# One half-load of V on ScalarE's queue, w_h ahead of the first rows of q, X's transposes ahead of a matmul group, and one half addition on GpSimd

## The chip, the cores and the metric

The kernel runs on one core of one Trainium2 chip. The core has five engines that run side by side and are tied together by semaphores: TensorE (PE, matmuls; its weight loads are shown apart as PEld), VectorE (DVE), ScalarE (ACT), GpSimd (POOL) and SyncE (SP), which here only issues transfers. Transfers between the chip's memory (HBM) and the core's own memory (SBUF) run on 16 DMA engines. They are issued from three queues: SP's, ACT's and POOL's. A load that changes the type on its way is issued from POOL.

The metric is device time in microseconds (us), the median of several executions, with the range beside it. One execution is also recorded by a profiler; its trace gives the start and length of every instruction.

## The reference

The reference is a windowed attention followed by a highway layer, in float32:

```python
keep = (pos_k < 4) | ((q_pos - k_pos >= 0) & (q_pos - k_pos < 128))
a = softmax(where(keep, q @ k.T / 8, -1e9))     # batch 4, heads 8, sequence 768, head size 64
x = (a @ v) as [3072, 512]                       # batch and sequence, heads side by side
H = maximum(x @ w_h, 0)
T = 1 / (1 + exp(-(x @ w_t + b_t)))
out = T * H + (1 - T) * x
```

Every query sees at most 128 keys up to itself, and the first four keys (the sinks).

## The kernel before

The 3072 rows are 24 tiles of 128 rows, six for each of four batches; a tile holds all 8 heads. For tile n these stages run:

- **scores** (`masks`, `product`, line 341): PE writes q times k of all heads, for the tile's keys and this and the next tile's queries, into one PSUM tensor `ps_s`, which is used again for every tile.
- **expo** (449): ACT takes the exponential of all of it into `E[n]`.
- **values** (460, 463): PE multiplies `E[n-1]` and `E[n]` with `v_of(n-1)` and `v_of(n)`, V in 16 bit with a column of ones, into `ps_av`.
- **norm** (480, 482): DVE divides by the sums and writes `X[n]`.
- **x_transpose** (498) and **x_copy** (503): PE transposes `X[n]` in four pieces into another part of `ps_av`, ACT copies them to `XT[n]`. For some tiles **sink_scores** (362), the scores of the sinks for several tiles, go into `ps_av` too, between the transposes and the copy.
- **gate** and **tanh** (508, 516): PE multiplies `XT[n]` with w_t into `ps_z`, ACT takes the tanh; **gate_value** (520 or 523) makes the sigmoid of it.
- **hidden** and **diff** (529, 542): PE multiplies `XT[n]` with w_h into `ps_h`, DVE computes max(H, 0) - X into `DD[n]`. There is one `ps_h`, so `hidden` of one tile waits for `diff` of the tile before.
- **gated** (547) multiplies `DD[n]` with the gate on DVE, **added** (553) adds X, on POOL for most tiles and on DVE for the last ones, and **store** (557) sends the tile out.

The stages of several tiles are interleaved by hand in one loop over n: turn n does scores and expo of tile n, values, norm and transposes of tile n-1, and gate and hidden of tile n-2. The order in which the program issues the instructions is the order on each engine (`_keep_traced_order`): an instruction that waits holds up all behind it on its engine, the issues of transfers among them.

Before q and k can be multiplied they are loaded by POOL in 16 bit into `nat` (`load_part`, line 117), in parts of 32 partitions, four parts (g = 0 to 3) to a segment of q or k, and DVE transposes a segment in blocks into `tr` (`transpose_qk`, line 133). The parts of batch 1's first segment are four of q (the first issued ahead of the loop, the others in turn 2) and four of k (turn 2). Their transposes stand in turns 4 (q) and 5 (k), and the scores of tile 6, the first of batch 1, need both.

V is loaded in 32 bit by SP, one transfer of 256 KB to a tile (`load_v`, line 140), into one of eight buffers; in turns up to 5 the transfer waits for the last matmul of the turn's scores (`after`). A cast brings V to 16 bit: on DVE for tiles 0 to 5 (`cast_v`, line 150), later mostly on POOL. V of tile 4 is loaded in turn 3, cast in turn 4 and used by `values(4)` in turn 5.

w_t and w_h are one transfer each on POOL's queue; w_h (line 644) is issued just ahead of the loop, behind the first part of batch 1's q (line 643). Its first user is `hidden(0)`, which turn 4 holds.

In turn 4 the order is: scores, `expo(4)`, `gate_value(0)`, `values(3)`, `norm(3)`, `gate(2)`, `tanh(2)`, `hidden(0)`, `diff(0)`, the transpose of batch 1's q, `cast_v(4)`, `gated(0)`, `added(0)`, more loads, then `x_transpose(3)`, `sink_scores` and `x_copy(3)` (lines 716 to 735). Turn 5 has the scores of tile 5 first, then `hidden(1)`, then `values(4)`.

After the loop the last tiles are finished one after the other. The last tile, 23, is done in two halves of 256 columns (lines 787 to 802): for each half gate, tanh, gate_value, hidden, diff, gated and `finish` (added and store). The left half is stored by SP, the right by ACT. Between the two, tile 22 is summed on PE and copied by ACT (line 798), and SP stores it (line 799).

Of the kernel before, what the change touches and what calls it, by code (L numbers as in the profile page):

```python
# [37 lines left out]
def kernel(  # L38
# [83 lines left out]
    def load_rows(b, i, which, gs=range(G)):  # L122
        for g in gs:
            load_part(b, i, g, which)
# [9 lines left out]

    V32 = [None] * N

    def load_v(n, after=None):
        b, t = divmod(n, NC)
        V32[n] = work.tile([P, H, D], FP32, tag="V32", name="V32", bufs=8)
        ins = sp.dma_start(out=V32[n],  # L140
                           in_=v[b, :, t * P:(t + 1) * P, :].transpose([1, 0, 2]))
        if after is not None:
            tc.add_manual_dep(
                ins.ins, after.ins.name,
                mybir.DependencyInfo(
                    mybir.DependencyClass.Sync, mybir.DependencyReason.DATA),
                reason="behind the loads needed first")

    def cast_v(n, engine):
        engine.tensor_copy(out=v_of(n)[:, :, 0:D], in_=V32[n])  # L150
# [144 lines left out]
    def sink_values(b, heads=slice(0, H)):  # L295
        if heads.start == 0:
            pool.tensor_copy(out=vs32[64:P, b, 0:D], in_=vs32[0:64, b, 0:D])
        shape = [P, heads.stop - heads.start, D + 1]
        pool.tensor_tensor(
            out=vs[b][:, heads], in0=vs32[:, b].unsqueeze(1).to_broadcast(shape),  # L300
            in1=vmask[:, heads].unsqueeze(2).to_broadcast(shape), op=ALU.mult)
# [101 lines left out]
    def opening(n, n1, n0):  # L403
        t = n1 % NC if n1 is not None else -1
        first = 0 if t >= 4 else 2
        todo = []

        def columns(half):
            b, c = divmod(n, NC)
            q1 = 2 * P if c + 1 < NC else P  # L410
            return q1 - K2 if half else min(q1, 2 * P if c == 0 else 3 * K2)

        for g in range(G):
            for half in range(2):
                split = n0 is not None and n is not None and 7 <= n < N - 1
                when = 256 if split and g == first + 1 - half else 0
                for u in range(4) if n is not None else ():
                    todo.append((when, len(todo), product, (n, u, g, half)))
                    when += columns(half)
                if n0 is not None and g == first + half:  # L420
                    if not split:
                        todo.append((when, len(todo), bias, (n0, g, half, 0)))
                    todo.append((when + 10 * P if split else when + 256, len(todo),
                                 bias, (n0, g, half, 1)))
                if t >= 2 and g // 2 == 1 - first // 2:
                    todo.append((when + 1 if split else when + 257, len(todo), sinks, (n1, g % 2, half)))
        ahead_of = []
        if n is not None:
            masks(n)
            for half in range(2) if n0 is not None and 7 <= n < N - 1 else ():  # L430
                ahead_of.append(bias(n0, first + 1 - half, half, 0))
        if ahead_of:
            passed = act.nop()
            behind(passed, ahead_of[-1])
        last = None
        for _, _, function, args in sorted(todo, key=lambda x: x[:2]):
            ins = function(*args)
            last = ins if function is product else last
            if function is bias and ahead_of:
                behind(ins, passed)  # L440
        return last
# [198 lines left out]
    cast_v(0, dve)  # L640
    sink_keys(0, dve)
    sink_values(0)
    load_rows(1, 0, 0, range(1))
    pool.dma_start(out=wh, in_=moe_w_h.rearrange("(kc p) of -> p kc of", p=P))

    idle(18)
    last = N - 1
    for n in range(last):

        nb, n1 = n - 2, n - 1  # L650
        joined = n < 5 or n >= 7
        before = (n1 if 0 <= n1 < N else None, nb if nb >= 0 else None)
        if n < N:
            after = opening(n, *before) if joined else scores(n)
            expo(n)
            if n in (4, 5):
                gate_value(n - 4)
            if n > NC and n % NC == NC - 1:
                gate_value(n - 3)
            for m in v_at.get(n, ()):  # L660
                if m < N:
                    load_v(m, after if n < 6 else None)
            if n % NC == (3 if n < NC else 1) and n // NC + 1 < B:
                load_sinks(n // NC + 1)
        if 5 <= n <= 6:
            hidden(1 if n == 5 else 3)
        if n == 0:
            idle(5)
        if not joined:
            opening(None, *before)  # L670
        if 0 <= n1 < N:
            values(n1)
        for m in cast_by_pool.get(n, ()):
            cast_v(m, pool)
        if n in late:
            finish(late[n])
        if NC <= n < N and n % NC == 0:
            sink_keys(n // NC)
        if n == 2:
            load_rows(1, 0, 0, range(1, G))  # L680
            load_rows(1, 0, 1)
        if n > NC and (n + 2) // NC < B and n % NC >= NC - 2:
            half = n % NC - (NC - 2)
            sink_values((n + 2) // NC, slice(G * half, G * half + G))
        if n != 4:
            load_parts(n)
        if n == NC + 1:
            sink_values(1)

        done = list(completed.get(n, ()))  # L690
        if n == 6:
            store(0)
            complete(done.pop(0))
        turn = list(units.get(n, ()))
        if 5 <= n <= 6:
            diff(1 if n == 5 else 3)
        if n == 7:
            cast_v_alone(7)
        if 0 <= n1 < N:
            norm(n1)  # L700
        if n == 3:
            transpose_qk(0, 2, 1, slice(0, 1))
            transpose_qk(0, 2, 1, slice(1, 2))
        if n == 2:
            transpose_qk(0, 2, 0)
        if n == 1:
            transpose_qk(0, 1, 1)
        if 0 < n < 4:
            cast_v(n, dve)
        for unit in turn if n != 4 else ():  # L710
            transpose_qk(*unit)

        if nb >= 0:
            gate(nb)
            tanh(nb)
        if n == 4:
            hidden(0)
            diff(0)
            transpose_qk(*turn.pop())
            cast_v(n, dve)  # L720
            gated(0)
            added(0)
            load_parts(n)
        if n == 5:
            gate_value(2)
            hidden(2)
        if n == 1:
            idle(3)
        if 6 <= n <= N:
            hidden(nb, range(KC // 2))  # L730
        if 0 <= n1 < N:
            x_transpose(n1)
            if n in sinks_at:
                sink_scores(*sinks_at[n])
            x_copy(n1)
            if n in sinks_at:
                sink_expo(*sinks_at[n])
            if nb >= N - 4:
                gate_value(nb)
        if 6 <= n <= N:  # L740
            hidden(nb, range(KC // 2, KC))
        if n in ahead:
            gate_value(ahead[n], pool)
        if n == last - 1:
            cast_v(last, pool)
        for m in done[:-1]:
            complete(m)
        if n == 5:
            diff(2)
            cast_v(n, dve)  # L750
        if 6 <= n <= N:
            diff(nb)
        for m in done[-1:] if n < last - 1 else ():
            complete(m)
# [32 lines left out]
    for part, cols, h, queue in ((0, left, h_left, sp), (1, right, ps_h[:, right], act)):  # L787
        gate(last, cols, gate_of(last, part))
        tanh(last, cols, gate_of(last, part))
        gate_value(last, cols=cols)  # L790
        hidden(last, cols=cols, into=h)
        if part == 1:

            for i, x in enumerate((flat(X[last - 1], slice(0, DM)), DD[last - 1])):
                pe.matmul(o_sum, lhsT=ident, rhs=x, start=(i == 0), stop=(i == 1),
                          skip_group_check=True)
            O[last - 1] = work.tile([P, DM], FP32, tag="O", name="O")
            act.copy(out=O[last - 1], in_=o_sum)
            sp.dma_start(out=out[(last - 1) * P:last * P, :], in_=O[last - 1])
        diff(last, cols, h)  # L800
        gated(last, cols)
        finish(last, cols, dve, queue)

    _keep_traced_order(tc)
# [33 lines left out]
```

## Time and profile before

| | |
|---|---|
| median of three runs | 106.77 us (106.72 to 108.35) |
| the profiled execution, its own time | 107.31 us |
| its span, first to last instruction | 105.3 us |
| PE busy | 94.1 us, 89% of the span |
| DVE busy | 86.4 us, 82% |
| ACT busy | 80.0 us, 76% |
| POOL busy | 83.5 us, 79% |
| read from HBM, written | 21.05 MB, 6.29 MB |

The rows that the next part quotes are of these kinds. A row of the timeline has the start in us from the span's start, the length in us, the engine and line, the operation with what it writes and reads, how many such instructions follow each other, and in brackets the idle time of the engine just before, with what ended it. Engine names with a q (SPq, ACTq) are issues of transfers. A row of transfers has what is moved, the queue, the count, KB of each and the median time in us from issue to landing. A row of queues has packets, MB and the time that the packets took, as a share of 16 engines' time in that window. A row of groups has the operation, its count, and after the bar the total busy time in us, the mean in ns, and the idle time before. Matmuls are pipelined and their ends modelled: consecutive matmuls overlap in the rows.

### The profile page before, as it was taken

The page shows a single profiled execution, that of the slowest core. Times are in us where ns is not written, and L with a number is a line of the kernel's source. Part 1 is how long each engine was busy: PE and PEld are TensorE (multiplying, and loading weights), DVE is VectorE, ACT ScalarE, POOL GpSimd, SP SyncE. Part 2 cuts the span into 40 slices and gives each one's busy share as a digit, 9 for nine tenths or more (in the row PEclk, how much of TensorE's full clock was granted, in tenths as well). Part 3 has the DMA queues.
Part 4 walks back from the last instruction along what each step waited for, and adds up shares of the span by engine and source line. Part 5 has one row for each costly group of instructions (what it writes and reads, how often), then busy time and mean ns, then how long its engine had stood idle before and what let it go on. Part 6 is the DMA issues. An engine that isn't in the chain of part 4 may idle for free. (4 is left out here: it accounts for less than half of the span.)

```text
span 105.3 us, 4691 instructions
## 1 busy us (share of the span) xinstructions
PE 94.1 (89%) x1960; PEld 52.4 (50%) x1960; DVE 86.4 (82%) x189; ACT 80.0 (76%) x105; POOL 83.5 (79%) x140
## 2 busy tenths in 40 slices
PE   5966786888999999999999999999999999999930
PEld 2323363454555545655565565554665656464610
DVE  6888755564896999899988996899889979999960
ACT  3297588687967499789778996897689978976750
POOL 6899709964998998897999999989978869768000
PEclk9999999999999999999999999999999999999995
DMA  2999999799999999989989999999996966252523
GB/s 54 229 237 238 185 207 224 99 175 197 230 222 253 209 261 202 182 163 207 237 188 219 203 217 230 207 241 283 219 242 157 270 187 218 106 199 103 202 93 107
DMA packets 36388, 20.81 MB, mean 198 GB/s; under 512 B 27020, under 2 KB 32912, under 8 KB 36368
## 3 DMA queue, kind: packets, MB, share of 16 engines
q1 hardware_dynamic: 29216, 13.31, 47.6%
q0 software_dynamic: 6848, 6.82, 42.0%
q10 hardware_dynamic: 304, 0.39, 1.3%
q8 instruction: 15, 0.25, 1.0%
q14 instruction: 5, 0.04, 0.2%
HBM read 21.05 MB, written 6.29 MB: 260 GB/s over the span
## 5 line engine op out<-in xcount | busy, mean ns | idle before, releaser
L449 ACT ACTIVATE E<-ps_s,ebias 128x2048 f16<-128x2048 f32 (+1 forms) x24 | 43.8, 1825 | 12.0 <-PE ps_s L341 12.0
L133 DVE STREAM_TRANSPOSE tr<-nat 128x384 f32<-128x384 f32 (+2 forms) x29 | 26.4, 937 | 1.6 <-DMA nat<-in_q_dram 1.2
L529 PE MATMUL ps_h<-wh,XT 128*128 128x512 f16 (+1 forms) x96 | 27.2, 375 | 0.5 <-DMA wh<-in_moe_w_h_dram 0.5
L553 POOL TENSOR_TENSOR O<-DD,X 128x512 f32<-128x512 f16 x19 | 22.0, 1157 | 5.6 <-DVE DD L547 3.8
L117 POOL DMA_DIRECT2D nat<-in_k_dram x40 | 21.8, 548 | 3.7 <-DMA wt<-in_moe_w_t_dram 2.6
L508 PE MATMUL ps_z<-wt,XT 128*128 128x512 f16 (+1 forms) x96 | 24.2, 374 | 0.1
L117 POOL DMA_DIRECT2D nat<-in_q_dram x32 | 17.8, 560 | 3.2 <-DMA wh<-in_moe_w_h_dram 2.2
L542 DVE SCALAR_TENSOR_TENSOR DD<-ps_h,X 128x512 f16<-128x512 f32 (+1 forms) x24 | 16.2, 674 | 4.8 <-PE ps_h L529 4.3
L341 PE MATMUL ps_s<-tr 32*64 32x192 f16 (+3 forms) x768 | 16.0, 243 | 2.5 <-DVE tr L133 2.3
L482 DVE TENSOR_TENSOR X<-ps_av,rec 128x512 f16<-128x512 f32 x23 | 15.9, 692 | 0.8
L516 ACT ACTIVATE TH<-ps_z 128x512 f16<-128x512 f32 (+1 forms) x24 | 14.0, 581 | 2.4 <-PE ps_z L508 2.4
L503 ACT COPY XT<-ps_av 128x512 f16<-128x512 f16 x23 | 13.5, 586 | 2.7 <-PE ps_av L498 1.1
L463 PE MATMUL ps_av<-v,E 128*128 128x65 f16 x184 | 13.5, 194 | 0.2 <-DVE v L150 0.2
L379 PE MATMUL ps_z<-brow,ones 32*64 32x256 f16 x94 | 12.7, 278 | 0.1
L341 PEld LDWEIGHTS <-tr 32*64 32x64 f16 x768 | 10.8, 104 | 3.7 <-DVE tr L133 2.0
L529 PEld LDWEIGHTS <-XT 128*128 128x128 f16 x100 | 8.7, 98 | 7.0 <-issue 1.0
L460 PE MATMUL ps_av<-v,E 128*128 128x65 f16 x152 | 12.0, 194 | 0.0
L463 PEld LDWEIGHTS <-E 128*128 128x128 f16 x192 | 11.7, 97 | 0.5
L460 PEld LDWEIGHTS <-E 128*128 128x128 f16 x160 | 10.2, 97 | 3.2 <-issue 1.8
L150 POOL CAST v<-V 128x512 f16<-128x512 f32 x17 | 11.3, 665 | 0.0
L508 PEld LDWEIGHTS <-XT 128*128 128x128 f16 x100 | 8.3, 98 | 5.9 <-issue 0.4
L547 DVE TENSOR_TENSOR DD<-DD,TH 128x512 f16<-128x512 f16 (+1 forms) x23 | 9.8, 427 | 0.8
(91 smaller groups left out, 112.4 us busy)
## 6 DMA issues: line engine op xcount, KB each, us to landing
V<-in_v_dram SPq DMA_DIRECT2D x24, 256.0 KB, 6.3
out_dram<-O SPq DMA_DIRECT2D x23, 256.0 KB, 3.1
nat<-in_k_dram POOLq DMA_DIRECT2D x24, 64.0 KB, 5.0
nat<-in_q_dram POOLq DMA_DIRECT2D x16, 96.0 KB, 4.7
nat<-in_k_dram POOLq DMA_DIRECT2D x16, 96.0 KB, 4.4
nat<-in_q_dram POOLq DMA_DIRECT2D x16, 64.0 KB, 5.5
first<-in_q_dram SPq DMA_DIRECT2D x6, 128.0 KB, 4.2
wt<-in_moe_w_t_dram POOLq DMA_DIRECT2D x1, 512.0 KB, 7.8
```

Source lines behind the costliest of these rows:

```text
L117: engine.dma_start(out=into[32 * g:32 * g + 32].rearrange("p hg m d -> p hg (m d)"), in_=(q, k)[which][b, :, t0:t0 + nt, :].rearrange("(hg ...
L133: dve.transpose(out=dst, in_=src)
L341: return pe.matmul(ps_s[ks, g, hg, q0:q1], lhsT=tr[b][rows, 1, hg, k0:k0 + K2, e], rhs=tr[b][rows, 0, hg, c * P + q0:c * P + q1, e], start ...
L449: act.activation(out=E[n][:, :, :, 0:nq * P], in_=ps_s[:, :, :, 0:nq * P], func=AF.Exp, bias=ebias, scale=SCALE)
L460: pe.matmul(slot, lhsT=E[n - 1][:, g, hg, P:2 * P], rhs=v_of(n - 1)[:, h, :], start=first, stop=False, skip_group_check=True)
L463: pe.matmul(slot, lhsT=E[n][:, g, hg, 0:P], rhs=v_of(n)[:, h, :], start=first, stop=True, skip_group_check=True)
L482: dve.tensor_tensor(out=X[n], in0=av[:, :, :, 0:D], in1=rec.unsqueeze(3).to_broadcast([P, HG, G, D]), op=ALU.mult)
L508: pe.matmul(into, lhsT=XT[n][:, kc * P:(kc + 1) * P], rhs=wt[:, kc, cols], start=False, stop=(kc == KC - 1), skip_group_check=True)
L516: act.activation(out=TH[n][:, cols], in_=ps_z if z is None else z, func=AF.Tanh, scale=0.5)
L529: pe.matmul(into, lhsT=XT[n][:, kc * P:(kc + 1) * P], rhs=wh[:, kc, cols], start=(kc == 0), stop=(kc == KC - 1), skip_group_check=True)
L542: dve.scalar_tensor_tensor(out=DD[n][:, cols], in0=ps_h[:, cols] if h is None else h, scalar=0.0, in1=flat(X[n], cols), op0=ALU.max, op1=A ...
L553: eng.tensor_tensor(out=O[n][:, cols], in0=DD[n][:, cols], in1=flat(X[n], cols), op=ALU.add)
```

## The change

Four edits. The first half of V's load of tile 4 (heads 0 to 3) stays with SP, at its old place behind tile 3's scores; the other half (heads 4 to 7) is issued by ACT, ahead of `expo(3)` and without that wait. `cast_v(4)` on DVE moves from behind the transpose of q to ahead of `diff(0)`. On POOL, w_h is issued ahead of the first part of batch 1's q, and in turn 4 PE does `x_transpose(3)` ahead of `hidden(0)` instead of behind it. For the last tile, the addition of the left half goes from DVE to POOL.

```diff
-    def load_v(n, after=None):
+    def load_v(n, after=None, heads=slice(0, H), queue=sp):
         b, t = divmod(n, NC)
-        V32[n] = work.tile([P, H, D], FP32, tag="V32", name="V32", bufs=8)
-        ins = sp.dma_start(out=V32[n],
-                           in_=v[b, :, t * P:(t + 1) * P, :].transpose([1, 0, 2]))
+        if V32[n] is None:
+            V32[n] = work.tile([P, H, D], FP32, tag="V32", name="V32", bufs=8)
+        ins = queue.dma_start(out=V32[n][:, heads],
+                              in_=v[b, heads, t * P:(t + 1) * P, :].transpose([1, 0, 2]))
...
     sink_values(0)
+    pool.dma_start(out=wh, in_=moe_w_h.rearrange("(kc p) of -> p kc of", p=P))
     load_rows(1, 0, 0, range(1))
-    pool.dma_start(out=wh, in_=moe_w_h.rearrange("(kc p) of -> p kc of", p=P))
...
             after = opening(n, *before) if joined else scores(n)
+            if n == 3:
+
+                load_v(4, heads=slice(H // 2, H), queue=act)
             expo(n)
...
                 if m < N:
-                    load_v(m, after if n < 6 else None)
+                    load_v(m, after if n < 6 else None,
+                           slice(0, H // 2) if m == 4 else slice(0, H))
...
         if n == 4:
+            cast_v(n, dve)
+            x_transpose(n1)
             hidden(0)
             diff(0)
             transpose_qk(*turn.pop())
-            cast_v(n, dve)
             gated(0)
...
         if 0 <= n1 < N:
-            x_transpose(n1)
+            if n != 4:
+                x_transpose(n1)
...
         gated(last, cols)
-        finish(last, cols, dve, queue)
+        finish(last, cols, (pool, dve)[part], queue)
```

## The prediction

> **What bounds the kernel now.** I read the windows first, to see which engine has no slack and where.
>
> ```profile
> span 105.3 us, 4691 instructions
> ...
> 24.00:36.00 12.00, 11.34 (x206) 5.95 (x205) 9.45 (x17) 9.17 (x13) 10.01 (x18) 1.00 1.21 223
> 36.00:50.00 14.00, 13.91 (x343) 8.01 (x336) 13.04 (x24) 11.77 (x14) 12.62 (x23) 1.00 1.07 205
> 50.00:70.00 20.00, 19.79 (x476) 11.49 (x468) 17.74 (x37) 16.75 (x19) 19.70 (x31) 1.00 1.02 219
> ```
>
> The columns after the window's length are the busy time of PE, weight loads, DVE, ACT and POOL. From 36 to 70 us PE is idle for 0.09 + 0.21 us in all. So whatever starts the steady part earlier should move its end by as much, as long as POOL (0.30 us idle from 50 to 70) can follow; POOL has 2.0 us to spare from 24 to 36. From 24 to 36 PE is idle for 0.66 us: that is about all the early edits can win.
>
> The timeline of PE says where these 0.66 us lie.
>
> ```profile
> 24.82 1.02 PE L529 MATMUL ps_h<-wh,XT 128*128 128x512 f16 x4 [0.47 <-DMA wh<-in_moe_w_h_dram]
> 25.68 0.39 PE L498 MATMUL ps_av<-ident,X 128*128 128x128 f16 x4
> ...
> 26.83 1.04 PE L529 MATMUL ps_h<-wh,XT 128*128 128x512 f16 x4
> ...
> 28.13 0.20 PE L460 MATMUL ps_av<-v,E 128*128 128x65 f16 x1
> 28.52 0.19 PE L463 MATMUL ps_av<-v,E 128*128 128x65 f16 x1 [0.19 <-DVE v L150]
> ...
> 28.98 1.02 PE L508 MATMUL ps_z<-wt,XT 128*128 128x512 f16 x4
> ...
> 31.32 0.43 PE L341 MATMUL ps_s<-tr 32*64 32x256 f16 x16
> ```
>
> 0.47 us is `hidden(0)` waiting for w_h, 0.19 us is `values(4)` waiting for the cast of V of tile 4. The second one costs more than its bracket: the next matmul starts 0.39 us after the first, where its row lasts 0.2 us. Now DVE in the same stretch.
>
> ```profile
> 23.84 0.69 DVE L482 TENSOR_TENSOR X<-ps_av,rec 128x512 f16<-128x512 f32 x1
> 25.88 0.69 DVE L542 SCALAR_TENSOR_TENSOR DD<-ps_h,X 128x512 f16<-128x512 f32 x1 [1.35 <-PE ps_h L529]
> 26.73 1.11 DVE L133 STREAM_TRANSPOSE tr<-nat 128x512 f32<-128x512 f32 x1 [0.16 <-DMA nat<-in_q_dram]
> 28.04 0.43 DVE L150 CAST v<-V 128x512 f16<-128x512 f32 x1 [0.20 <-DMA V<-in_v_dram]
> ...
> 30.16 1.10 DVE L133 STREAM_TRANSPOSE tr<-nat 128x512 f32<-128x512 f32 x1
> ```
>
> DVE sat idle for 1.35 us before `diff(0)` at 25.88, and then ran almost without a gap to 30.16; the transpose at 30.16 (k of batch 1) ends at 31.26, and PE's scores of tile 6 begin at 31.32. Two resources are thus level there, and both must come earlier. Last the transfers that feed this.
>
> ```profile
> 17.77 0.60 POOL L117 DMA_DIRECT2D nat<-in_q_dram  x1
> 18.37 0.77 POOL L644 DMA_DIRECT2D wh<-in_moe_w_h_dram  x1
> 19.13 1.59 POOL L117 DMA_DIRECT2D nat<-in_q_dram  x3
> 20.71 2.10 POOL L117 DMA_DIRECT2D nat<-in_k_dram  x4
> 25.06 0.53 POOL L117 DMA_DIRECT2D nat<-in_q_dram  x1 [2.24 <-DMA wh<-in_moe_w_h_dram]
> ```
> ```profile
> 19.42 0.37 SPq L140 DMA_DIRECT2D V<-in_v_dram  x1
> ```
> ```profile
> wh<-in_moe_w_h_dram POOLq DMA_DIRECT2D x1, 512.0 KB, 6.4
> V<-in_v_dram SPq DMA_DIRECT2D x1, 256.0 KB, 8.6
> ```
> ```profile
> q0 software_dynamic: 506, 0.51, 116.7%
> ```
>
> w_h lands at 18.37 + 6.4 = 24.77, V of tile 4 at 19.42 + 8.6 = 28.02. The last row is the whole list of queues between 20.5 and 23.5 us: only POOL's queue moves, V on SP's queue gets no packet beside w_h. So V's 8.6 us are 4.1 us of standing still and 4.5 us of moving 256 KB beside other loads.
>
> **The change part by part.**
>
> *w_h first.* It is issued at 17.77 in place of 18.37, 0.6 us sooner, and lands at about 24.2; the first part of q moves behind it, with the same bytes ahead of the later parts as now. One thing moves with it. The rows above show seven issues behind w_h (x3, x4) and the eighth waiting for w_h to land (24.77, issue at 25.06). With q's first part now behind w_h too, the eighth is the last part of k, which was issued at about 22.3. It will go out at 24.2 + 0.3 = 24.5.
>
> ```profile
> nat<-in_k_dram POOLq DMA_DIRECT2D x1, 64.0 KB, 7.3
> ```
> ```profile
> nat<-in_k_dram POOLq DMA_DIRECT2D x24, 64.0 KB, 5.0
> ```
>
> That part took 7.3 us and was there at 29.6; all parts of this size took 5.0 in the median. From 24.5 it lands between 29.5 and 31.8. I take 29.5, the median: its 7.3 us were spent behind w_h and six other parts, most of which will be through.
>
> *Half of V by ACT.*
>
> ```profile
> 19.43 1.97 ACT L449 ACTIVATE E<-ps_s,ebias 128x2048 f16<-128x2048 f32 x1 [1.18 <-PE ps_s L341]
> ```
> ```profile
> L140 SPq DMA_DIRECT2D V<-in_v_dram x24: 368/528/2154, 5.3 to 84.2; - x24
> ```
> ```profile
> out_dram<-O ACTq DMA_DIRECT2D x1, 128.0 KB, 1.9
> ```
>
> ACT is idle from 18.25 to 19.43, so an issue of 0.37 us is hidden; at the longest seen on SP, 2.15 us, `expo(3)` behind it would start 0.97 us late. ACT's one 128 KB store landed in 1.9 us, so this half lands between 20.2 and, with V's own 8.6 us, 26.9. I take the early end, since 18.25 is ahead of w_h's packets. SP's half is still issued at 19.42. w_h's stretch ends 0.6 us sooner, so it waits until 22.9 and then moves: alone, half of 4.5 us, landing at 25.15; if ACT's half is still moving beside it, up to 4.5 us, landing at 27.4. I take 25.15.
>
> The Trainium skill, "DMA: Bandwidth & Descriptors", section "Queues, rings and completion order", says that each DMA engine takes turns between queues, but switches only at the end of a packet of at most 64 descriptors. The 506 packets of one queue fit a long turn of w_h, not short ones. Its "Rules for kernel authors" say that spreading transfers over issuing engines brings no bandwidth; by that, both halves together would land no sooner than whole V, and the time would be that of the second rival below.
>
> *The new order of tile 4.* X of tile 3 is done at 23.84 + 0.69 = 24.53. PE transposes it from 24.59 (0.06 us behind DVE, as at 31.32; 0.39 us), `hidden(0)` runs from 24.98 to 26.00, w_h being there since 24.2. On DVE the cast goes from 25.15 to 25.6, inside the 1.35 us that were idle, so `diff(0)` starts at 26.0 and ends at 26.7; `hidden(1)` starts at 26.75 instead of 26.83: 0.08 us. `values(4)` no longer stands for the cast: 0.39 less 0.04 for a matmul's own step, 0.35 us. PE is 0.43 us ahead at `gate(3)`. DVE loses the cast and its wait between 27.84 and 28.45, so the transpose of k moves from 30.16 to about 29.55; PE needs its end at 31.32 - 0.43 - 0.06, its start by 29.75, which 29.5 for k's last part allows. Gain of the stage: about 0.4 us.
>
> *GpSimd adds up the last left half.*
>
> ```profile
> 96.26 1.15 POOL L553 TENSOR_TENSOR O<-DD,X 128x512 f32<-128x512 f16 x1 [0.36 <-DVE DD L547]
> ```
> ```profile
> 95.75 0.43 DVE L547 TENSOR_TENSOR DD<-DD,TH 128x512 f16<-128x512 f16 x1
> ...
> 96.88 0.81 DVE L547 TENSOR_TENSOR DD<-DD,TH 128x512 f16<-128x512 f16 x1
> ...
> 100.14 0.29 DVE L547 TENSOR_TENSOR DD<-DD,TH 128x256 f16<-128x256 f16 x1
> 100.47 0.43 DVE L553 TENSOR_TENSOR O<-DD,X 128x256 f32<-128x256 f16 x1
> 100.81 0.42 DVE L542 SCALAR_TENSOR_TENSOR DD<-ps_h,X 128x256 f16<-128x256 f32 x1
> 101.34 0.29 DVE L547 TENSOR_TENSOR DD<-DD,TH 128x256 f16<-128x256 f16 x1
> ```
> ```profile
> L299 POOL TENSOR_TENSOR vs<-vs,vmask 128x260 f16<-128x260 f32 x4 | 2.5, 619 | 0.2
> ```
> ```profile
> 101.58 0.33 SPq L799 DMA_DIRECT2D out_dram<-O  x1
> 102.12 0.37 ACTq L557 DMA_DIRECT2D out_dram<-O  x1
> ```
>
> DVE drops the 0.43 us at 100.47, and `diff` of the right half can start there, 0.34 us sooner than 100.81. No row shows a POOL add 256 wide: it lies between half of 1.15 us (0.58) and all of it; I take 0.62, by the 260-wide product. The add at 96.26 began 0.08 us behind the product that ended at 96.18, so this one runs from 100.51 to about 101.14. The product at 96.88, beside a POOL add, took 0.81 us in place of 0.43 and ended 0.28 us after POOL did (97.41). So `gated` of the right half, ready at 100.95, ends at about 101.14 + 0.28 = 101.42 at worst, against 101.63 now, and the right store goes out at 101.9 in place of 102.12: 0.2 us. The left store leaves at 101.2 in place of 100.93 and is off SP by 101.55, just ahead of the store at 101.58. Bounds: with POOL at 1.15 us, `gated` ends at 101.95 and SP's store of tile 22 leaves at 102.05: a loss of 0.3 to 0.5 us; without any blocking a gain of 0.35.
>
> *Sum.* 0.4 + 0.2 = 0.6 us. The profiled execution took 107.31 us (its span of 105.3 and 2.0 around it), the median of the three runs is 106.77; taken off both, 106.7 and 106.2.
>
> **Rivals.**
> 1. *Only the tail wins.* k's last part, held behind w_h, lands at 30.0 or later. The transpose then ends no sooner than 31.1 and PE keeps 0.1 us or nothing: 106.77 - 0.2 = 106.6. For it: 7.3 us in place of 5.0; against: the median of 5.0, and that six other parts and w_h are ahead of it by then.
> 2. *Slower: V holds DVE.* The cast now stands ahead of `diff(0)`. If V lands at T, the cast ends at T + 0.45, `diff(0)` at T + 1.15, `hidden(1)` starts at T + 1.2, and `gate(3)` follows 28.98 - 26.83 - 0.35 = 1.8 us behind: T + 3.0. The break-even is T = 26.0; each us beyond costs a us. At 27.4 it is 1.4 - 0.2 = 1.2 us: 108.0; at 26.5 it is 0.3: 107.1. I price it at 107.5. Against it: SP's half is a half.
> 3. *POOL's add is slow.* At its upper bound the tail loses 0.4 in place of winning 0.2: 106.8 with the early gain.
> 4. *The early edits do not do what they say*, because ACT's issue takes 2 us: 106.77 + 0.97 - 0.2 = 107.5.
>
> **How the numbers follow.** Forecast 106.2 (105.8 to 106.5): 0.53; rival 1: 0.19; rival 2: 0.19; rival 3: 0.05; rival 4: 0.04. From 105.8 (0.7 us in the stage's idle time plus 0.35 at the tail, less rounding) to 107.5, half of rival 2, about 0.85 is held. A measurement of this kernel tells about 2%, 2.1 us, from no change. Faster by that: 0.01, since all idle time touched is about 1 us. Slower by that needs V after 28: 0.03. Within: 0.96.
>
> **What would show it.** Right: no bracket with w_h before `hidden(0)`; the two matmuls around 28.1 at 0.04 us apart; the cast on DVE between `norm(3)` and `diff(0)`, with `diff(0)` released by PE; k's last part issued near 24.5; `gated` of the right half longer than 0.29 us and the last store near 101.5 on the new clock. Wrong: `diff(0)` starting right behind the cast, released by V's transfer; the transpose of k released by its transfer; ACT's issue beyond 1.2 us; a POOL add of 0.9 us or more.

## The result and the profile after

The changed kernel is slower: 112.52 us in the median (110.19 to 113.15, six executions) against 106.97 (106.20 to 108.35, six) for the kernel before. The ratio is 1.034, interval [1.026, 1.043]; here and below a ratio compares only those executions of each kernel that lie within 1.5% of its fastest, while the medians hold all. Forecast were 106.2 us and no measurable change. The profiled execution took 110.55 us, 3.2 more than that of before; its span is 3.0 longer. Four of the six executions took 112.42 to 113.15, and what made up their further 2 us no kept trace shows: what follows explains the 3 us between the two profiled executions, not the 5.5 us between the medians. Executions of one kernel differ by 2 us and more, so what follows rests on ratios and on the waits in the traces, not on one time against another.

The page's head and the windows of the changed kernel (columns as before) already say where the 3 us are not.

```profile
span 108.3 us, 4694 instructions
...
PE   5976785987999998999999999999999999999200
...
POOL 6899529939799899479999999999976697780200
...
24.00:36.00 12.00, 11.12 (x212) 5.91 (x217) 9.17 (x17) 9.03 (x13) 11.37 (x23) 1.00 1.20 224
36.00:50.00 14.00, 13.52 (x316) 7.71 (x309) 13.02 (x24) 11.45 (x12) 11.12 (x18) 1.00 0.96 182
50.00:70.00 20.00, 19.90 (x477) 11.72 (x477) 17.90 (x38) 17.05 (x20) 19.82 (x32) 1.00 1.03 219
```

PE is busy for 94.1 us in both kernels, and within 0.4 us of before in each of these stretches, but the last two of 40 slices (2.7 us each) are empty of all computing, where before only the last one was. The time is lost behind the last instruction. The tail's own rows of the changed kernel (timeline, several engines) are nearly as forecast:

```profile
100.59 0.67 POOL L554 TENSOR_TENSOR O<-DD,X 128x256 f32<-128x256 f16 x1 [3.12 <-DVE DD L548]
...
101.10 0.32 DVE L548 TENSOR_TENSOR DD<-DD,TH 128x256 f16<-128x256 f16 x1
101.29 0.33 SPq L558 DMA_DIRECT2D out_dram<-O  x1
101.44 0.42 DVE L554 TENSOR_TENSOR O<-DD,X 128x256 f32<-128x256 f16 x1
101.72 0.38 SPq L806 DMA_DIRECT2D out_dram<-O  x1
101.90 0.37 ACTq L558 DMA_DIRECT2D out_dram<-O  x1
```

GpSimd's add took 0.67 us (0.62 forecast), the right store went out at 101.90 (101.9 forecast; 102.12 before). What stands behind it is seen only when one asks for the source line that closes the program, 833 before and 840 after. Each engine has DRAIN rows there, of which the trace gives the start and the length. The rows hold the count, the shortest, median and longest in ns, and the first and last start in us. First the kernel before, then the changed one:

```profile
L833 POOLq EVENT_SEMAPHORE  x4: 17/17/17, 104.6 to 105.2; - x4
L833 POOLq DRAIN  x3: 46/107/7407, 96.2 to 105.1; - x3
L833 SPq DRAIN  x3: 7/7/7, 104.5 to 104.8; - x3
```
```profile
L840 POOLq EVENT_SEMAPHORE  x4: 17/17/17, 107.5 to 108.2; - x4
L840 POOLq DRAIN  x3: 46/107/6923, 100.6 to 108.0; - x3
L840 SPq DRAIN  x3: 7/7/13, 104.6 to 107.7; - x3
```

Before, GpSimd's first DRAIN runs from 96.2 for 7.41 us to 103.6, while GpSimd's last addition (96.26, 1.15 us) had ended at 97.41: the DRAIN ends 6.2 us behind it. SP's first DRAIN, behind the last store, is at 104.5, so the 6.2 us lay under the tail with 0.9 to spare. After, the last addition ends at 101.26, the DRAIN at 107.5, again 6.2 us later, and all engines wait for it: SP was ready at 104.7, 2.8 us earlier.

Now the early stage. The timeline of PE in the changed kernel:

```profile
24.44 0.40 PE L499 MATMUL ps_av<-ident,X 128*128 128x128 f16 x4 [0.24 <-DVE X L483]
24.68 1.03 PE L530 MATMUL ps_h<-wh,XT 128*128 128x512 f16 x4
...
27.17 1.02 PE L530 MATMUL ps_h<-wh,XT 128*128 128x512 f16 x4 [0.64 <-DVE DD L543]
...
28.46 0.20 PE L461 MATMUL ps_av<-v,E 128*128 128x65 f16 x1
28.50 0.20 PE L464 MATMUL ps_av<-v,E 128*128 128x65 f16 x1
...
28.95 1.02 PE L509 MATMUL ps_z<-wt,XT 128*128 128x512 f16 x4
```

and of DVE, followed by the issues of ACT, POOL and SP; then, in the view of transfers, w_h and SP's half of V (KB, us from issue to landing):

```profile
23.69 0.69 DVE L483 TENSOR_TENSOR X<-ps_av,rec 128x512 f16<-128x512 f32 x1
26.05 0.48 DVE L151 CAST v<-V 128x512 f16<-128x512 f32 x1 [1.67 <-DMA V<-in_v_dram]
26.45 0.67 DVE L543 SCALAR_TENSOR_TENSOR DD<-ps_h,X 128x512 f16<-128x512 f32 x1
...
17.57 0.40 ACTq L141 DMA_DIRECT2D V<-in_v_dram  x1
...
17.33 0.82 POOL L644 DMA_DIRECT2D wh<-in_moe_w_h_dram  x1
...
23.64 0.53 POOL L117 DMA_DIRECT2D nat<-in_k_dram  x1 [1.81 <-DMA wh<-in_moe_w_h_dram]
...
19.27 0.37 SPq L141 DMA_DIRECT2D V<-in_v_dram  x1
```
```profile
wh<-in_moe_w_h_dram POOLq DMA_DIRECT2D x1, 512.0 KB, 6.0
...
V<-in_v_dram SPq DMA_DIRECT2D x1, 128.0 KB, 6.7
```

`hidden(0)` no longer waits for w_h (landed 23.3), and `values(4)` no longer for the cast: its two matmuls are 0.04 us apart. But the cast, now ahead of `diff(0)`, waits 1.67 us for SP's half of V, which lands at 19.27 + 6.7 = 25.97 instead of 25.15; `diff(0)` stands behind it, and `hidden(1)` waits 0.64 us for the one `ps_h`. `gate(3)` starts at 28.95, before at 28.98. In this execution the early edits are worth nothing, and the 3.0 us of the span are 2.8 of DRAIN and 0.14 at SP's last store (101.72 for 101.58).

### The profile page after: what moved, and what is told of

Same layout as the page of the kernel before. It is cut to its first block, busy times and chain, and to the rows that moved or that the text cites. A ratio compares the mean times of both kernels' runs of the same rounds, so it can differ in the third digit from the quotient of the medians.

```text
span 108.3 us, 4694 instructions
## 1 busy us (share of the span) xinstructions
PE 94.1 (87%) x1960; PEld 52.3 (48%) x1960; DVE 86.2 (80%) x188; ACT 79.9 (74%) x105; POOL 83.8 (77%) x141
## 5 line engine op out<-in xcount | busy, mean ns | idle before, releaser
L554 POOL TENSOR_TENSOR O<-DD,X 128x512 f32<-128x512 f16 (+1 forms) x20 | 22.7, 1135 | 10.4 <-DVE DD L548 8.5
L509 PE MATMUL ps_z<-wt,XT 128*128 128x512 f16 (+1 forms) x96 | 24.2, 374 | 0.0
L117 POOL DMA_DIRECT2D nat<-in_q_dram x32 | 17.3, 548 | 0.4 <-DMA nat<-in_q_dram 0.4
L461 PEld LDWEIGHTS <-E 128*128 128x128 f16 x160 | 10.1, 97 | 2.9 <-issue 1.5
```

Source lines behind the costliest of these rows:

```text
L117: engine.dma_start(out=into[32 * g:32 * g + 32].rearrange("p hg m d -> p hg (m d)"), in_=(q, k)[which][b, :, t0:t0 + nt, :].rearrange("(hg ...
L461: pe.matmul(slot, lhsT=E[n - 1][:, g, hg, P:2 * P], rhs=v_of(n - 1)[:, h, :], start=first, stop=False, skip_group_check=True)
L509: pe.matmul(into, lhsT=XT[n][:, kc * P:(kc + 1) * P], rhs=wt[:, kc, cols], start=False, stop=(kc == KC - 1), skip_group_check=True)
L554: eng.tensor_tensor(out=O[n][:, cols], in0=DD[n][:, cols], in1=flat(X[n], cols), op=ALU.add)
```

## The experiments

Two theories. *The end:* GpSimd's DRAIN follows its last instruction by 6.2 us whatever that was; one more instruction there moves the end as soon as it ends later than 0.9 us behind the last of before. Its rival: the addition itself, its port or the stores delay the end. *The start:* the cast ahead of `diff(0)` makes DVE and then PE wait for V. Its rival: w_h first, or ACT's half, costs something on the queues. Only three ratios lie above 2% with their whole interval: those of the change, of the addition alone and of the copy in the left half. The smaller ones are read together with the waits in the traces beside them.

**The two halves of the change apart.** First the change without the GpSimd addition:

```diff
-        finish(last, cols, (pool, dve)[part], queue)
+        finish(last, cols, dve, queue)
```

> The changed kernel with the last left half added on DVE again; the three early edits stay. Theory A (the program's end waits for GpSimd: its closing DRAIN, the row of 6.92 us that starts at 100.56 in the changed kernel and 7.41 us at 96.22 in the kernel before, ends 6.22 us after GpSimd's last add in both, at 107.48 and 103.63): the DRAIN ends near 103.7 again, ahead of SP's last wait near 104.6, and the time goes back to 106.5 to 107.3. Rival B (the early edits lose it: V late, the cast ahead of diff(0), a collision of DVE and POOL at tile 9): the time stays at 109.5 to 110.6.

Measured 108.65 us (107.78 to 109.56), ratio to before 1.017 [1.012, 1.022]: between the two expectations. GpSimd's DRAIN ends ahead of SP again (table below), as theory A has it, and 1.7% is left, as rival B has it. Then the GpSimd addition alone, on the kernel before:

```diff
-        finish(last, cols, dve, queue)
+        finish(last, cols, (pool, dve)[part], queue)
```

> The kernel before with the last left half added on GpSimd and nothing else. Theory A: GpSimd's last add ends near 101.2, its DRAIN near 107.4 in place of 103.6, and the last semaphore of GpSimd moves from 104.57 to 107.4: 2.9 us longer, 109.4 to 110.2. Rival B: within 0.4 us of the kernel before, 106.5 to 107.2.

Measured 110.34 us (108.70 to 112.20), ratio 1.030 [1.022, 1.038], at the upper end of what theory A gave. So both halves lose, the addition the more: 3.0% and 1.7% make 4.7%, a little above the whole (3.4%, up to 4.3%). The 1.7% probably varies with the landing of V, which was harmless in the changed kernel's own trace. In the trace of the addition alone, its last row on GpSimd and the closing rows:

```profile
100.47 0.67 POOL L553 TENSOR_TENSOR O<-DD,X 128x256 f32<-128x256 f16 x1 [3.10 <-DVE DD L547]
```
```profile
L833 POOLq DRAIN  x3: 46/107/6923, 100.4 to 107.9; - x3
L833 SPq DRAIN  x3: 7/7/13, 104.6 to 107.6; - x3
```

100.4 + 6.92 = 107.3, again 6.2 us behind the addition's end, and 2.8 us later than SP.

**Is it the addition, or any instruction?** A copy of one column, whose result nobody reads, was put on GpSimd, on the kernel before, at three places; the DVE addition stays.

```diff
+    spare = const.tile([P, 1], FP16, tag="spare")
...
         gated(last, cols)
+        if part == 0:
+            pool.tensor_copy(out=spare, in_=DD[last][:, 0:1])
```

> The kernel before with one more GpSimd instruction, a copy of one column behind the gated product of the last tile's left half; DVE still adds. Theory A (any late GpSimd instruction puts off the DRAIN's end): the copy ends near 100.7, the DRAIN near 106.9, 2.4 us longer: 108.9 to 109.6. Rival C (it is the half-tile addition itself, its length or its hold on DVE): a copy of 0.1 us costs nothing, 106.5 to 107.2.

Measured 112.00 us (111.17 to 112.91), ratio 1.049 [1.043, 1.055].

```diff
     gated(last - 1)
+    pool.tensor_copy(out=spare, in_=DD[last - 1][:, 0:1])
```

> The same copy of one column, but behind the gated product of tile 22, which ends at 99.54 in the kernel before. Theory A with a fixed 6.2 us: the copy ends near 99.75, the DRAIN near 106.0, 1.4 us past 104.57: 107.9 to 108.6. Rival C, and a theory by which only work behind tile 23 matters: 106.5 to 107.2.

Measured 110.03 us (108.67 to 112.41), ratio 1.023 [1.017, 1.029].

```diff
     complete(last - 2)
+    pool.tensor_copy(out=spare, in_=DD[last - 2][:, 0:1])
```

> The kernel before with the copy of one column on GpSimd behind the gated product of tile 21, which ends at 97.69 there. Theory A with the fixed 6.22 us: the copy ends by 98.1, the DRAIN by 104.3, still ahead of SP's last wait at 104.54: no change, 106.3 to 107.3. Rival C2 (one more GpSimd instruction near the end costs about 2 us wherever it stands): 108.5 to 109.5.

Measured 109.41 us (107.17 to 110.83), ratio 1.011 [1.004, 1.017]. The first two times lie above what theory A gave, and the third in the range of rival C2, by which one more GpSimd instruction costs about 2 us wherever it stands; the DRAIN explains 0.2 us of the third (table below). The new tile `spare` was suspected, so the middle place was run again with an old tile as target, and the tile was run alone, filled once by DVE and used by nobody.

```diff
     gated(last - 1)
+    pool.tensor_copy(out=past, in_=DD[last - 1][:, 0:1])
```

> The kernel before with a copy of one column on GpSimd behind the gated product of tile 22, written into a tile that is there anyway, so that no address in SBUF moves. Theory A: the copy ends about 0.2 us after that product, GpSimd's DRAIN 6.22 us later, and its last semaphores come 1.2 to 1.5 us behind SP's DRAIN: 1.2 to 1.5 us above the kernel before. Rival C: no difference, 0.3 us at most.

Measured 109.99 us (108.29 to 111.25; before on that chip 108.14), four executions and no interval. Its trace, the timeline and the closing rows:

```profile
98.98 0.19 POOL L784 CAST past<-DD 128x1 f32<-128x1 f16 x1 [2.21 <-DVE DD L547]
```
```profile
L834 POOLq DRAIN  x3: 46/107/6427, 99.0 to 105.9; - x3
L834 SPq DRAIN  x3: 7/7/13, 103.8 to 105.7; - x3
```

A copy of 0.19 us on an otherwise idle engine ends at 99.17; the DRAIN ends at 105.4, 1.5 us after SP was ready.

```diff
+    spare = const.tile([P, 1], FP16, tag="spare")
...
+    dve.memset(spare, 0.0)
```

> The kernel before with one more tile of one column, cleared once by DVE at the start (0.06 us), and nothing on GpSimd. If moving the addresses of the tiles behind it is what put the three kernels with a one-column copy some us later before tile 23 than their DRAIN explains: 1 us or more above the kernel before. If that was the run-to-run spread of the early loads: within 0.5 us.

Measured 109.01 us (108.32 to 109.95), ratio 1.015 [1.009, 1.021]; the medians, with 108.14 for before, differ by 0.9 us or 0.8%. So the kernel with a tile of two bytes in each partition was about 1% slower, and the times of the three kernels above hold that as well. The copy behind tile 21 is then no slower than the tile alone (1.011 and 1.015), which speaks against rival C2; the copy in the left half still lies 3.4% above it, where its DRAIN explains 2.6 us, and that rest stays open. The DRAIN readings do not depend on the tile. All of them together, from the same rows of each trace (us):

| kernel | GpSimd's last instruction ends | its DRAIN ends | SP's DRAIN starts | GpSimd later than SP by |
|---|---|---|---|---|
| before | 97.4 | 103.6 | 104.5 | -0.9 |
| the change without the addition | 97.9 | 104.1 | 105.0 | -0.8 |
| copy behind tile 21 | 100.9 | 107.1 | 106.9 | 0.2 |
| copy behind tile 22, new tile | 103.3 | 109.5 | 108.0 | 1.5 |
| copy behind tile 22, old tile | 99.2 | 105.4 | 103.9 | 1.5 |
| copy in the left half | 102.0 | 108.3 | 105.6 | 2.6 |
| addition alone | 101.1 | 107.4 | 104.6 | 2.8 |
| the change | 101.3 | 107.5 | 104.7 | 2.8 |

The second column less the first is 6.2 us in all eight, for instructions of 0.19, 0.44, 0.67, 0.71 and 1.15 us, and in the six other traces too; the later the instruction stands, the more of it shows. The rival, that the addition itself, its port or the stores delay the end, falls: the copies touch neither the stores nor DVE's work. What GpSimd does in the 6.2 us the traces do not show.

**What of the early edits costs.** All that follow are without the GpSimd addition. The trace of the first experiment, DVE and PE:

```profile
26.87 0.43 DVE L151 CAST v<-V 128x512 f16<-128x512 f32 x1 [2.63 <-DMA V<-in_v_dram]
...
27.95 1.02 PE L530 MATMUL ps_h<-wh,XT 128*128 128x512 f16 x4 [1.56 <-DVE DD L543]
```

V holds the cast for 2.63 us and PE for 1.56: the second rival of the prediction. Three variants of that kernel. All of V issued by ACT, which removes SP's late half:

```diff
-                load_v(4, heads=slice(H // 2, H), queue=act)
+                load_v(4, queue=act)
...
-                if m < N:
-                    load_v(m, after if n < 6 else None,
-                           slice(0, H // 2) if m == 4 else slice(0, H))
+                if m < N and m != 4:
+                    load_v(m, after if n < 6 else None)
```

> The changed kernel with the last add on DVE and all of V of tile 4 issued by ACT at about 17.6, ahead of tile 3's scores; none of it waits for them. Theory B2 (what the early edits lose is SP's half of V, landing at 26.0 to 26.8 behind w_h, with the cast ahead of diff(0)): V lands by 24.5, the cast ends by 25.2, hidden(1) has no wait for diff(0) and the time is 106.0 to 106.8, at or below the kernel before. Rival D (the loss is k's last part behind w_h, or the order of X's transposes): it stays at 107.8 to 109.5.

Measured 108.42 us (107.92 to 109.08), ratio 1.014 [1.009, 1.019]; the 106.0 to 106.8 expected was missed, and the rival's range was met. V was there in time, but w_h took 7.6 us. On GpSimd and PE of that trace:

```profile
25.71 0.53 POOL L117 DMA_DIRECT2D nat<-in_k_dram  x1 [3.44 <-DMA wh<-in_moe_w_h_dram]
...
37.37 0.62 POOL L151 CAST v<-V 128x512 f16<-128x512 f32 x1
...
38.05 0.42 PE L464 MATMUL ps_av<-v,E 128*128 128x65 f16 x8 [1.37 <-POOL v L151]
```

The eighth issue behind w_h stood for 3.44 us, GpSimd ran late, and 12 us further on PE waited 1.37 us for a cast of V by GpSimd: the exponential of tile 7 came at 36.66 (before: 36.79), that of tile 8 at 41.21 (39.98). The wait was not removed, it moved. That this chain is the whole 1.4% was not tested.

The cast back at its old place, with the halves, w_h first and X's transposes ahead of `hidden(0)` kept:

```diff
         if n == 4:
-            cast_v(n, dve)
             x_transpose(n1)
             hidden(0)
             diff(0)
             transpose_qk(*turn.pop())
+            cast_v(n, dve)
```

> The changed kernel with the last add on DVE and the cast of tile 4 at its old place, behind the transpose of q; V still in two halves. Theory B2: V at 26.0 to 26.8 is then in time for the cast near 27.8, diff(0) is held by nothing, values(4) does not wait: 106.0 to 106.9. Rival D: 107.8 to 109.5.

Measured 107.37 us (105.93 to 110.69) beside 107.46 for before: ratio 1.002 [0.996, 1.007]. Its DVE and PE:

```profile
23.07 0.69 DVE L483 TENSOR_TENSOR X<-ps_av,rec 128x512 f16<-128x512 f32 x1
25.12 0.69 DVE L543 SCALAR_TENSOR_TENSOR DD<-ps_h,X 128x512 f16<-128x512 f32 x1 [1.35 <-PE ps_h L530]
25.73 1.10 DVE L133 STREAM_TRANSPOSE tr<-nat 128x512 f32<-128x512 f32 x1
26.67 0.41 DVE L151 CAST v<-V 128x512 f16<-128x512 f32 x1
...
27.65 1.03 PE L509 MATMUL ps_z<-wt,XT 128*128 128x512 f16 x4
```

No wait for V: `diff(0)` waits for PE alone, and the cast finds V there. Last, the V edits alone, on the kernel before, with w_h and X's transposes in their old order:

```diff
+            if n == 3:
+                load_v(4, heads=slice(H // 2, H), queue=act)
...
+            cast_v(n, dve)
             hidden(0)
             diff(0)
             transpose_qk(*turn.pop())
-            cast_v(n, dve)
```

> The kernel before with V of tile 4 in two halves and the cast ahead of diff(0); w_h and X's transposes in the old order. Theory B2: w_h goes out 0.6 us later again and SP's half stands behind it for longer, V lands near 27, hidden(1) waits 1 to 2 us for diff(0): 107.8 to 109.5. Rival D: 106.3 to 107.2.

Measured 108.53 us (107.27 to 112.47), ratio 1.011 [1.004, 1.017]. In its trace the cast waits 2.91 us for V and `hidden(1)` 1.17. The cast ahead of `diff(0)` loses with the new order of w_h and without it.

**The same pair again, side by side on another chip.** The change without the addition,

> The changed kernel with the last add on DVE, beside the next one on the same chip. Theory E (the cast ahead of diff(0) makes PE wait for V through DVE whenever V lands after about 26): 1.0 to 2.0 us above the kernel before, with a wait of hidden(1) for diff(0) of 0.6 us or more. Rival F (the early edits are neutral and the distance seen came from the chip): within 0.5 us of the kernel before.

109.31 us (108.34 to 111.06), ratio 1.015 [1.008, 1.023]; the cast waited 3.36 us, `hidden(1)` 2.15. And with the cast back,

> The same kernel with the cast of tile 4 behind the transpose of q, its old place. Theory E: 1.0 to 1.6 us below its neighbour with the cast ahead, and within 0.5 us of the kernel before. Rival F: the two are equal within 0.5 us.

107.30 us (105.69 to 108.28), ratio 0.992 [0.985, 0.998]. The one move of the cast is worth 2.0 us of the median there; in the first round, where the two kernels stood on different chips, their ratios are 1.5% apart. What is left of the change, halves and w_h first, is level with before to 0.8% better; the two intervals agree only in part, so a gain is not settled.

A late V cost more in that trace than the wait. PE had stood idle for 2.15 us, and the share of its clock that was granted to it fell to 0.65 from 29 to 30 us and to 0.50 from 30 to 32, from 1.00 before and again from 33: the four matmuls of `gate(3)` took 1.90 us in place of 1.02. Behind the 1.56 us of the first experiment it stayed at 1.00.

**How steady the early stage is.** From X of tile 3 on DVE to `gate(3)` on PE, worked out from the same two rows of each trace, with the us that w_h and V of tile 4 took (for halves: SP's half):

| kernel | X of 3 to gate(3) | w_h | V |
|---|---|---|---|
| before | 5.14 | 6.4 | 8.6 |
| addition alone (early order of before) | 4.57 | 6.5 | 8.0 |
| copy behind tile 22, old tile (same) | 4.64 | 6.2 | 8.3 |
| three copies with the new tile, tile alone (same) | 4.85, 8.07, 6.84, 6.38 | 6.9, 8.3, 7.5, 7.1 | 8.3, 10.5, 10.3, 10.1 |
| the change | 5.26 | 6.0 | 6.7 |
| the change without the addition, first and second | 6.19, 7.52 | 6.5, 7.0 | 7.8, 8.4 |
| all of V by ACT | 5.23 | 7.6 | no wait |
| V edits alone | 6.51 | 6.8 | 7.9 |
| cast back, first and second | 4.58, 5.90 | 6.4, 7.8 | 7.9, 9.3 |

The order of before does the stage in 4.57 us where w_h and V come a little sooner. The 0.47 + 0.19 us of waits that the edits aimed at are thus mostly one execution's luck with its loads: the two next rows have no wait for w_h at all.

## Why the prediction was wrong

**The tail: the step that failed most.** The forecast took GpSimd's part of the tail to be the 0.62 us of its addition, and the end to be the last store. Left out was GpSimd's closing DRAIN, 6.2 us behind its last instruction and with 0.9 us to spare before. The addition moved that last instruction from 97.41 to 101.26, by 3.85 us: 3.85 - 0.9 = 2.95; the span grew by 3.0, and alone the addition costs 3.0% [2.2, 3.8], 3.2 us of 106.8. The row stands in the trace of the kernel before, but busy time, chain of waits and groups do not count it. Rival 3 had the right edit with the wrong reason, a slow addition (it took 0.67 us), and so the wrong price, 0.4 us.

**The right store, even without that.** It did go out 0.22 us sooner, `gated` taking 0.32 us beside the addition. But SP's DRAIN came 2.96 us behind SP's store of tile 22 in both traces (101.58 and 104.54, 101.72 and 104.68), while the right store moved from 0.54 to 0.18 us behind that store. In all fourteen traces SP's DRAIN comes 2.9 to 3.0 us behind SP's last store. So SP's end followed that store, which left 0.14 us later: 0.07 because ACT's copy of tile 22, which it sends out, ended later (101.62 for 101.55), the rest, it seems, because the left store stood on SP until 101.62. In place of a gain of 0.2 us there was a loss of about 0.1. That order was in the forecast ("just ahead of the store at 101.58"), with no price.

**V: the rival that came true.** SP's half was put at 25.15, "alone, half of 4.5 us" behind w_h; it landed at 25.97 here and at 26.75 in the first experiment, 6.7 to 9.3 us after its issue in six traces, where the whole tile had taken 8.0 to 8.6. Halving it saved at most 2 us. The mechanism and break-even of rival 2 (T = 26.0) hold: at 25.97 `gate(3)` came out level (28.95 against T + 3.0 = 28.97), at 26.75 it started at 29.73 (T + 3.0 = 29.75), and with the V edits alone, at 19.59 + 7.9 = 27.5, at 30.52 (30.5). In the second trace without the addition, at 18.75 + 8.4 = 27.15, it started at 30.77, 0.6 us behind T + 3.0, for there PE ran at the lower clock, which rival 2 had no price for. Its chance of 0.19 was the mistake. The prediction had cited the Trainium skill, "DMA: Bandwidth & Descriptors", section "Rules for kernel authors", that more issuing engines bring no bandwidth; by that, V's halves land no sooner than V whole. The traces come closer to that rule than to the sum.

**The gain of 0.4 us in the stage.** Its parts happened: w_h first (landed 23.3, 24.2 forecast), k's last part as the eighth issue (23.64, waiting for w_h), `values(4)` without its gap, ACT's issue at no cost (0.40 us beside `x_copy`), the transpose of k without a wait at 30.08, so that neither rival 1 nor rival 4 came true. But the waits removed were smaller in other executions of the old order, as the last table shows, so there was less to win.

**"Whatever starts earlier moves the end".** It did not. The exponentials of tiles 7, 8 and 9 on ACT, before and with the addition alone, whose early order is the old one:

```profile
36.79 1.97 ACT L449 ACTIVATE E<-ps_s,ebias 128x2048 f16<-128x2048 f32 x1 [0.78 <-PE ps_s L341]
39.98 1.97 ACT L449 ACTIVATE E<-ps_s,ebias 128x2048 f16<-128x2048 f32 x1 [0.26 <-PE ps_s L341]
44.00 1.97 ACT L449 ACTIVATE E<-ps_s,ebias 128x2048 f16<-128x2048 f32 x1 [0.49 <-PE ps_s L341]
```
```profile
35.58 1.97 ACT L449 ACTIVATE E<-ps_s,ebias 128x2048 f16<-128x2048 f32 x1 [0.61 <-PE ps_s L341]
39.72 1.97 ACT L449 ACTIVATE E<-ps_s,ebias 128x2048 f16<-128x2048 f32 x1 [0.61 <-PE ps_s L341]
43.95 1.97 ACT L449 ACTIVATE E<-ps_s,ebias 128x2048 f16<-128x2048 f32 x1 [0.49 <-PE ps_s L341]
...
36.55 0.42 PE L463 MATMUL ps_av<-v,E 128*128 128x65 f16 x8 [0.96 <-POOL v L150]
```

A lead of 1.21 us at tile 7 is 0.26 at tile 8, where PE waits 0.96 us for GpSimd's cast of V, and 0.05 at tile 9. In the changed kernel a lead of 0.25 us at tile 8 (39.73) is lost at tile 9 to a meeting of DVE and GpSimd (its rows, then those of before):

```profile
40.39 0.81 DVE L548 TENSOR_TENSOR DD<-DD,TH 128x512 f16<-128x512 f16 x1
...
39.87 1.05 POOL L300 TENSOR_TENSOR vs<-vs,vmask 128x520 f16<-128x520 f32 x1
```
```profile
40.47 0.41 DVE L547 TENSOR_TENSOR DD<-DD,TH 128x512 f16<-128x512 f16 x1
...
41.07 1.05 POOL L299 TENSOR_TENSOR vs<-vs,vmask 128x520 f16<-128x520 f32 x1
```

The product takes 0.81 us beside a GpSimd product and 0.41 where it meets only a small GpSimd copy (64x64, 0.48 us there and 0.23 in the changed kernel); the order in which the two meet changed, not their work. X behind it then starts at 41.36 in place of 41.04, PE waits for X, and tile 9's exponential comes at 44.31 in place of 44.00. The Trainium skill, "SBUF — State Buffer", section "Who interferes with whom", says that a DVE instruction with two SBUF inputs contends with a GpSimd instruction that reads SBUF; these rows agree. Not every lead is lost: with the cast back, tile 7 came at 35.24 and the end of its span 1.1 us before that of the kernel before. PE's idle 0.30 us in one trace showed no slack in that alignment of the engines, not that another alignment would have none.

## What to carry to other kernels

Ask for the rows of the line that closes the program before moving work to an engine at the end: an engine that has been idle for some us may have a closing step that lies hidden under that very idleness. Put no wait for a transfer ahead of an instruction that frees a shared buffer unless the transfer was early in several executions; a landing time read from one trace is a draw. Price the chance of a half load by the whole load's time, not by half of it, while other queues are full.

## What the runs showed of the hardware that was not expected

GpSimd's closing DRAIN ends 6.2 us after GpSimd's last instruction, in all fourteen traces, whether that took 0.19 or 1.15 us.

Where PE had waited 2.15 us (second trace without the addition) and 2.32 us (copy behind tile 22, new tile), the clock granted to it fell to 0.50 for two us and more; where it had waited up to 1.56 us, in the other traces, it stayed at 1.00.

A tile of two bytes per partition, filled once and never used, went with a kernel slower by 1.5% [0.9, 2.1], or by 0.8% between the medians. In three of four traces that hold it, V of tile 4 takes 10.1 to 10.5 us instead of 8.0 to 8.6, and in all four w_h takes 6.9 to 8.3 instead of 6.2 to 6.5. But w_h took 7.0 to 7.8 us in three traces without the tile as well, all with w_h issued first, so slow loads are not its mark alone. That the addresses of the tiles behind it matter to the loads is a guess that was not tested; the cause stays open. It also means that a part of what the early edits lose or win could come from such a shift, though they add no tile.
